# Scores over 512 keys on 64 partitions, and K transposed in halves, in a two-layer cached-attention decode kernel

## The chip, the cores and the metric

The kernel runs on one core of one Trainium2 chip. The metric is device time in microseconds (us), the median of several runs. Engines are named as the profile names them: PE is TensorE (PEld its weight loads), DVE is VectorE, ACT ScalarE, POOL GpSimd, SP SyncE, whose queue issues all the loads.

## The reference

One token of width 640 passes two equal layers, each an attention over a cache and a mixer. What the change touches is the attention's scores and softmax:

```python
Hq, Hkv, Sk, Dh = 32, 32, 32768, 192
W = min(4096, max(256, Sk // 4))                 # 4096 keys
q = (x @ wq).reshape(B, Sq, Hq, Dh)              # x after layernorm, one row
k = k_cache[:, :, Sk - W:, :]                    # bf16, 1.5 MB a head
v = v_cache[:, :, Sk - W:, :]
scores = einsum("bhqd,bhkd->bhqk", q, k) * Dh ** -0.5
p = softmax(scores, axis=-1)
o = einsum("bhqk,bhkd->bhqd", p, v)
x = x + o.reshape(B, Sq, Hq * Dh) @ wo
```

The mixer is layernorm, a product with w3, gelu and a product with w4 (for one token the shifted part of the reference is zero). Both layers read the same caches and weights.

## The kernel before

**Loads.** K and V of each head come as one load of 1.5 MB each into one of 12 cells in SBUF (`take`, `give`: a cell is free again when the work that reads it has been given). Loads go out in one fixed order (`layer_stream`, `need`) from SP; in the steady part up to eight are under way at once, and an issue waits for the landing of an earlier one or for its cell. wo, w3 and w4 use cells too. Layer 1 (layer 0 in the code) goes through the groups of four heads from the last to the first. Eight heads (0 to 7, `NKEEP`) keep their transposed K in cells for layer 2, which begins with them and loads no K for them.

**K transposed (L450).** K lies with keys on partitions, and TensorE needs Dh there. VectorE transposes 32x32 blocks of 4-byte words, so pairs of bf16. `transpose_quart` does a quarter of a head, 128x768 words; `T(h, half)` does two. The result goes to a kept cell, or to `area`, one cell that four quarters use in turn.

**Scores (L534).** `scores` multiplies the 16 columns of `Qblk` (four heads times four blocks of 32 rows, zero where another head's columns are) by the transposed K. Six products (three blocks of 64 of Dh, even and odd) add up in PSUM. Quarter q writes to partitions 32q to 32q+15, one strip of 32, over 256 columns: 24 matmuls a head, over two strips in turn for a half, over all four for a kept head. Four heads add into one tile of 128 partitions and 256 columns. Two such tiles lie beside each other in one PSUM bank (`ST_both`, `next_scores`), so that the scores of the next group are made while this group's softmax reads the other.

**Softmax steps.** `part_max` (L557) takes the maximum over the 256 columns, `turn_max` (L562) turns the 128 maxima into a row, `full_max` (L567, L572) reduces them to one per head and scales, `spread_max` turns that into a bias (L580, L583) and takes the exponential (L586) with its sums, `turn_p` (L591, L593) transposes the probabilities in 32x32 blocks, `swap` (L605, L608, L613) brings them to keys on partitions (PT) with 16 small matmuls and sums the denominators, and `recip` inverts those.

**Values.** `pv` (L655) makes 16 matmuls over the four strips per head; VectorE transposes the result (L662, `o_sb`), and `o_fold` (L669 to L675) sums it into the head's column of oT. `o_sb` is also the space of the softmax steps (`o_words`).

**Order.** The order on each engine is that in which the program is written; the semaphores between engines are placed by the framework. For a group, the prologue makes the first head of the next group: T of both halves with `part_max` between them, S of both halves with `turn_max` and `full_max` between, then the other steps, the query of the group after, and T of the second head. Then, for each head of this group, PV, T and S of one more head of the next group, and the fold. The last groups of a layer (`hurry`, `quick`) have the last softmax early. In layer 2's first group the steps stand between the kept heads' scores:

```python
between = [lambda: (turn_max(), full_max()), spread_max, turn_p, lambda: None]
for (q2, h2), step in zip(keep, between):
    for half in range(2):
        T(h2, half)
        S(h2, half, ST_n, q2)
    step()
```

For a kept head T does nothing, and S makes all 24 matmuls at once and gives the cell back.

Of the kernel before, what the change touches and what calls it, by code (L numbers as in the profile page):

```python
# [18 lines left out]
P = 128  # L19
# [40 lines left out]
def kernel(  # L60
# [30 lines left out]
    QT = QC // P  # L91
    NT = 4
    QUART = NFB * (NGK // NT) * P * 2
    FREE = NT * QUART
    scale = float(Dh) ** -0.5
# [336 lines left out]

    def transpose_quart(layer, h, q):

        if layer == 1 and h < NKEEP:
            return kept[h][:, q * QUART:(q + 1) * QUART]
        Kn = need("k", layer, h)
        NY = NFB * (NGK // NT)
        Ku = Kn[:].bitcast(U32).rearrange("p (j y b) -> p j y b", j=NJ4, b=32)
        if layer == 0 and h < NKEEP:  # L440
            if q == 0:
                kept[h] = take(("T", h))
            T = kept[h][:, q * QUART:(q + 1) * QUART]
        else:
            if area[0] is None:
                area[0] = take(("area", layer))
            T = area[0][:, area[1] * QUART:(area[1] + 1) * QUART]
            area[1] = (area[1] + 1) % NT
        Tu = T.bitcast(U32).rearrange("p (y j b) -> p j y b", y=NY, j=NJ4)
        nc.vector.transpose(Tu, Ku[:, :, q * NY:(q + 1) * NY])  # L450
        if q == NT - 1:
            give(("k", layer, h))
        return T

    def qproj_steps(c, xc, part=None, row=None):
# [29 lines left out]
        def spread():  # L485
            if row is not None:
                qT_ps = psm.tile([P, n], F32, tag="psm")
                for tl in range(n):
                    i, j = divmod(tl, n // 2)
                    nc.tensor.matmul(qT_ps[:, tl:tl + 1], lhsT=row[:, j * P:(j + 1) * P],  # L490
                                     rhs=Eq[0:33, i, 0:1], start=True, stop=True)
                held["q"] = qT_ps
            Xq = o_bytes[:, 2 * (SW + 2 * QH):][:, 0:4 * n].rearrange("p (t b) -> p t b", b=4)
            nc.vector.tensor_tensor(  # L494
                out=Xq[:], in0=held["q"][:, :].unsqueeze(2).broadcast_to([P, n, 4]),
                in1=maskq[:, :].unsqueeze(1).broadcast_to([P, n, 4]), op=ALU.mult)
            held["x"] = Xq
# [25 lines left out]

    def scores(h, Ts, q0, ST_ps, hq):

        ng = NGK // NT
        Q = [Qblk[:, h // QH % 2, QAT[hq] + n * QSTEP:][:, 0:QW] for n in range(NCOL)]
        views = [T.rearrange("p (g f i t) -> p g f i t", f=NFB, g=ng, i=P) for T in Ts]
        for f in range(NFB):
            for t in range(2):  # L530
                n = 2 * f + t
                for i, T4 in enumerate(views):
                    r = 32 * (q0 + i)
                    nc.tensor.matmul(  # L534
                        ST_ps[r:r + QW, :].rearrange("p (g i) -> p g i", g=ng), lhsT=Q[n],
                        rhs=T4[:, :, f, :, t],
                        start=(hq == 0 and n == 0), stop=(hq == QH - 1 and n == NCOL - 1))


    ST_both = psS.tile([P, 2 * SW], F32, name="ST_ps")  # L540
    nc.vector.memset(ST_both[:], 0.0)
    turn = [0]

    def next_scores():
        turn[0] += 1
        i = turn[0] % 2
        return ST_both[:, i * SW:(i + 1) * SW]

    def softmax_steps(n, ST_ps, sc, space, bank=None):
        held = {}
        halves = space.bitcast(BF16)

        def part_max():
            pm = short("pm")
            nc.vector.tensor_reduce(out=pm[:], in_=ST_ps, op=ALU.max, axis=AX.X)  # L557
            held["pm"] = pm

        def turn_max():  # L560
            pmT_ps = psm.tile([1, P], F32, tag="psm")
            nc.tensor.transpose(pmT_ps[0:1, :], held["pm"][:, 0:1], ident[:, :])  # L562
            held["pmT"] = pmT_ps

        def full_max():
            ngm = space[0:1, SW:SW + 2 * QH]
            nc.vector.tensor_reduce(out=ngm[:], in_=held["pmT"][0:1, :].rearrange("o (q x m) -> o x q m", q=4, m=NM),  # L567
                                    op=ALU.max, axis=AX.XY, negate=True)
            held["PrT"] = halves[:, SW:2 * SW]

            wide = held["PrT"][0:1, :].bitcast(F32)
            nc.vector.tensor_scalar(  # L572
                out=wide.rearrange("o (q x m) -> o q x m", q=4, m=NM),
                in0=ngm[:].unsqueeze(1).unsqueeze(3).broadcast_to([1, 4, 2 * QH, NM]),
                scalar1=sc[0:1, 0:1], scalar2=None, op0=ALU.mult)
            held["w"] = wide

        def spread_max():
            nb_ps = psm.tile([P, 1], F32, tag="psm")
            nc.tensor.matmul(nb_ps[:], lhsT=held["w"],  # L580
                             rhs=one[0:1, :], start=True, stop=True)
            nb_sb = space[:, 289:290]
            nc.scalar.copy(nb_sb[:], nb_ps[:])  # L583
            Pr = halves[:, 0:SW]
            lpart = space[:, 288:289]
            nc.scalar.activation(out=Pr, in_=ST_ps, func=ACTF.Exp,  # L586
                                 bias=nb_sb[:, 0:1], scale=sc[:, 0:1], accum_out=lpart[:, 0:1])
            held["Pr"], held["l"] = Pr, lpart

        def turn_p():  # L590
            nc.vector.transpose(held["PrT"], held["Pr"])  # L591
            lh = space[:, 280:284]
            nc.vector.tensor_scalar(out=lh[:], in0=hm[:], scalar1=held["l"][:, 0:1], scalar2=None, op0=ALU.mult)  # L593
            held["lh"] = lh

        def swap():
# [6 lines left out]
            for m in range(NM):  # L603
                for q in range(NT):
                    nc.tensor.matmul(PT_ps[32 * m:32 * (m + 1), :, :, ng * q:ng * (q + 1)], lhsT=Eq[:, q, :],  # L605
                                     rhs=src[:, m:QW:NM], start=True, stop=True)
# [4 lines left out]
            else:  # L611
                l_ps = bank[:, 512:512 + QH]
            nc.tensor.matmul(l_ps[:], lhsT=ones, rhs=held["lh"][:], start=True, stop=True)  # L613
            held["lps"] = l_ps
# [112 lines left out]
    def attention(layer, x_cur, rs_cur, x_new, z_new, rs_new, ss_new):  # L727
# [12 lines left out]

        def T(h, half):
            for q in (2 * half, 2 * half + 1):
                if (h, q) not in Th:
                    Th[h, q] = transpose_quart(layer, h, q)

        def S(h, half, ST_ps, hq):
            if layer == 1 and h < NKEEP:
# [3 lines left out]
                return  # L751
            scores(h, [Th.pop((h, q)) for q in (2 * half, 2 * half + 1)], 2 * half, ST_ps, hq)
            if half == 1 and layer == 0 and h == last_plain:
# [39 lines left out]
        for hq, h in enumerate(groups[0]):  # L793
            for half in range(2):
                if layer == 0:
                    T(h, half)
                else:
                    Th.update({(h, q): transpose_quart(layer, h, q) for q in (2 * half, 2 * half + 1)})
                S(h, half, ST, hq)
# [11 lines left out]
        def early_t(quarts):  # L811
            h, i = quarts.popleft()
            Th[h, i] = transpose_quart(layer, h, i)

# [321 lines left out]
```

## Time and profile before

| | |
|---|---|
| time, median of 3 runs | 511.49 us (511.09 to 511.76) |
| the profiled execution | 511.59 us, its span 509.8 us |
| PE busy | 317.2 us (62%), 4084 matmuls |
| DVE busy | 292.0 us (57%) |
| ACT busy | 48.9 us (10%) |
| read from HBM | 214.01 MB, 420 GB/s over the span |
| scores' matmuls (L534) | 1536 of 128x256, 365 ns each |
| K's transposes (L450) | 224 of 128x768 words, 945 ns each |
| TensorE clock granted, mean | 0.708 |

The span runs from the first instruction to the last. PE's busy time counts matmuls that run side by side once, and a matmul's own time holds its way through the array, so counts times means say little there. Where the text names a moment, it is in us from the span's start; layer 1 runs to about 286 us. In a row of the timeline the columns are start, length, engine, line, operation, operands and count; the bracket is the engine's idle time before it and what ended it.

### The profile page before, as it was taken

The page shows a single profiled execution, that of the slowest core. Times are in us where ns is not written, and L with a number is a line of the kernel's source. Part 1 is how long each engine was busy: PE and PEld are TensorE (multiplying, and loading weights), DVE is VectorE, ACT ScalarE, POOL GpSimd, SP SyncE. Part 2 cuts the span into 40 slices and gives each one's busy share as a digit, 9 for nine tenths or more (in the row PEclk, how much of TensorE's full clock was granted, in tenths as well). Part 3 has the DMA queues.
Part 4 walks back from the last instruction along what each step waited for, and adds up shares of the span by engine and source line. Part 5 has one row for each costly group of instructions (what it writes and reads, how often), then busy time and mean ns, then how long its engine had stood idle before and what let it go on. Part 6 is the DMA issues. An engine that isn't in the chain of part 4 may idle for free.

```text
span 509.8 us, 9498 instructions
## 1 busy us (share of the span) xinstructions
PE 317.2 (62%) x4084; PEld 188.0 (37%) x4084; DVE 292.0 (57%) x604; ACT 48.9 (10%) x173; POOL 3.7 (1%) x16
## 2 busy tenths in 40 slices
PE   1056677676566664767755777576565665657685
PEld 0023334334333332534433645343333333324354
DVE  2068557656774755566723276865575555756522
ACT  1000101010010100001010111010100101001111
POOL 2000000000000000000000000000000000000000
PEclk9999656557787776655675597957785967876655
DMA  9999999999999999999999999999999999999996
GB/s 370 432 432 430 429 441 432 437 429 419 420 426 433 432 427 448 432 404 459 422 396 414 370 435 429 443 429 440 426 422 424 429 422 432 428 446 429 415 409 246
DMA packets 12014, 214.63 MB, mean 421 GB/s; under 512 B 2564, under 2 KB 3076, under 8 KB 7428
## 3 DMA queue, kind: packets, MB, share of 16 engines
q1 hardware_dynamic: 11972, 214.02, 98.6%
q8 instruction: 32, 0.52, 0.4%
q14 instruction: 10, 0.08, 0.0%
HBM read 214.01 MB, written 0.00 MB: 420 GB/s over the span
## 4 chain that ended last, share of the span: by engine, by line
DMA 65%; PE 17%; DVE 12%; issue 3%; ACT 1%; SPq 1%; DVEq 0%; ACTq 0%
DMA cell<-in_A_k_cache_dram 43%; DMA cell<-in_A_v_cache_dram 18%; DVE cell L450 8%; PE ST_ps L534 8%; DMA cell<-in_B_w_dram 4%; PE O_ps L655 4%; DVE o_sb L662 1%; PE y_ps L1080 1%; DVE words L557 1%; PE qT_ps L480 1%; DVE V_ps L644 1%; PE nb_ps L580 1%; ACT o_sb L586 1%; PE l_ps L613 1%; SPq L55 0%
## 5 line engine op out<-in xcount | busy, mean ns | idle before, releaser
L534 PE MATMUL ST_ps<-cell,Qblk 128*16 128x256 bf16 x1536 | 158.2, 365 | 110.3 <-DVE cell L450 67.4
L450 DVE STREAM_TRANSPOSE cell<-cell 128x768 uint32<-128x768 uint32 x224 | 201.6, 945 | 33.4 <-DMA cell<-in_A_k_cache_dram 32.6
L534 PEld LDWEIGHTS <-Qblk 128*16 128x16 bf16 x1536 | 84.6, 108 | 176.7 <-issue 152.4
L655 PE MATMUL O_ps<-cell,PT 128*2 128x384 bf16 x968 | 94.8, 458 | 10.1 <-DMA cell<-in_A_v_cache_dram 8.2
L662 DVE STREAM_TRANSPOSE o_sb<-O_ps 128x384 f32<-128x384 f32 x62 | 35.4, 571 | 79.7 <-PE O_ps L655 79.7
L655 PEld LDWEIGHTS <-PT 128*2 128x2 bf16 x1024 | 43.6, 98 | 25.7 <-issue 17.7
L670 ACT ACTIVATE words<-oT_ps,words 32x6 bf16<-32x6 f32 x40 | 10.3, 257 | 163.3 <-PE oT_ps L669 151.5
L591 DVE STREAM_TRANSPOSE o_sb<-o_sb 128x256 bf16<-128x256 bf16 x15 | 6.7, 445 | 30.7 <-ACT o_sb L586 24.2
L669 PE MATMUL oT_ps<-o_sb,Lq 128*32 128x6 f32 x160 | 13.3, 192 | 10.0 <-DVE o_sb L662 9.4
L669 PEld LDWEIGHTS oT_ps<-o_sb,Lq 128*32 128x32 f32 x160 | 11.7, 137 | 18.5 <-issue 11.6
L675 ACT ACTIVATE words<-oT_ps,words 32x6 bf16<-32x6 f32 x24 | 6.2, 257 | 114.8 <-PE ST_ps L534 90.5
L494 DVE TENSOR_TENSOR o_sb<-qT_ps,words 128x24 bf16<-128x24 f32 (+1 forms) x18 | 3.0, 164 | 22.0 <-PE qT_ps L480 17.0
L480 PE MATMUL qT_ps<-words,wq_sb 128*128 128x1 bf16 x210 | 7.0, 165 | 13.0 <-DMA wq_sb<-in_A_wq_dram 12.1
L469 PE MATMUL qr_ps<-wq_sb,words 128*1 128x384 bf16 x90 | 13.6, 454 | 0.0
L480 PEld LDWEIGHTS <-wq_sb 128*128 128x128 bf16 x210 | 6.6, 100 | 14.2 <-DMA wq_sb<-in_A_wq_dram 13.2
L583 ACT COPY o_sb<-nb_ps 128x1 f32<-128x1 f32 x15 | 2.4, 159 | 93.3 <-PE nb_ps L580 93.3
L605 PEld LDWEIGHTS <-ident 128*32 128x32 bf16 x256 | 5.9, 113 | 12.2 <-issue 12.0
L701 PE MATMUL yr_ps<-cell,words 128*1 128x320 bf16 x108 | 10.0, 325 | 0.0
L674 PE MATMUL oT_ps<-o_sb,Lq 128*32 128x6 f32 x48 | 6.1, 200 | 6.0 <-DVE o_sb L673 5.8
L674 PEld LDWEIGHTS oT_ps<-o_sb,Lq 128*32 128x32 f32 x48 | 5.5, 143 | 10.5 <-issue 9.7
L580 PEld LDWEIGHTS nb_ps<-words,o_sb 1*128 1x128 f32 x30 | 6.6, 273 | 6.4 <-issue 5.6
L683 PE MATMUL y_ps<-words,cell 128*128 128x1 bf16 x210 | 7.1, 166 | 2.5 <-issue 1.4
(161 smaller groups left out, 205.6 us busy)
## 6 DMA issues: line engine op xcount, KB each, us to landing
cell<-in_A_k_cache_dram SPq DMA_DIRECT2D x56, 1536.0 KB, 27.7
cell<-in_A_v_cache_dram SPq DMA_DIRECT2D x56, 1536.0 KB, 27.7
cell<-in_A_wo_dram SPq DMA_DIRECT2D x13, 960.0 KB, 27.7
wq_sb<-in_A_wq_dram SPq DMA_DIRECT2D x5, 1536.0 KB, 13.4
cell<-in_A_v_cache_dram SPq DMA_DIRECT2D x6, 768.0 KB, 23.6
cell<-in_B_w_dram SPq DMA_DIRECT2D x1, 1536.0 KB, 11.8
cell<-in_B_w_dram SPq DMA_DIRECT2D x2, 768.0 KB, 10.3
cell<-in_A_wo_dram SPq DMA_DIRECT2D x3, 480.0 KB, 17.0
```

The source lines that it names most:

```text
L450: nc.vector.transpose(Tu, Ku[:, :, q * NY:(q + 1) * NY])
L469: nc.tensor.matmul(qr_ps[32 * i:32 * i + 1, :], lhsT=xc[:, kc:kc + 1], rhs=wq_sb[:, kc, t0 * P + i * N:t0 * P + (i + 1) * N], start=(kc == ...
L480: nc.tensor.matmul(qT_ps[:, tl:tl + 1], lhsT=wq_sb[:, kc, t * P:(t + 1) * P], rhs=xc[:, kc:kc + 1], start=(kc == 0), stop=(kc == ND - 1))
L534: nc.tensor.matmul(ST_ps[r:r + QW, :].rearrange("p (g i) -> p g i", g=ng), lhsT=Q[n], rhs=T4[:, :, f, :, t], start=(hq == 0 and n == 0), s ...
L580: nc.tensor.matmul(nb_ps[:], lhsT=held["w"], rhs=one[0:1, :], start=True, stop=True)
L655: nc.tensor.matmul(O_ps[r:r + 2, :], lhsT=PT[:, hq, 2 * i:2 * i + 2], rhs=v_pair(V, h, 2 * i * Dh, 2 * Dh), start=(i < 4), stop=(i >= NB - 4))
L662: nc.vector.transpose(o_sb[:], O_ps.rearrange("p (e a c) -> p e c a", e=2, c=NA))
L669: nc.tensor.matmul(oT_ps[r, :], lhsT=Lq[:], rhs=o_sb[:, e, :, e], start=(e == 0), stop=(e == 1))
L670: nc.scalar.activation(oT[r, :], oT_ps[r, :], ACTF.Copy, scale=rl[r, 0:1])
L674: nc.tensor.matmul(oT_ps[r, :], lhsT=Lq[:], rhs=o2, start=True, stop=True)
L683: nc.tensor.matmul(y_ps[:, n:n + 1], lhsT=wo_t[:, k * D + n * P:k * D + (n + 1) * P], rhs=oT[:, k:k + 1], start=(i == 0), stop=(i == len(o ...
L701: nc.tensor.matmul(yr_ps[32 * i:32 * i + 1, :], lhsT=oT[:, k:k + 1], rhs=wo_t[:, k * D + i * N:k * D + (i + 1) * N], start=(k == 0), stop= ...
```

## The change

A head's K is transposed in two halves of 128x1536 words (`transpose_half`, `NT = 2`) where it was four quarters of 128x768. A half's scores are six matmuls of 512 columns to one strip of 32 PSUM partitions, where they were twelve of 256 columns over two strips; a kept head has twelve over two strips, where it had 24 over four. A group's scores lie on 64 partitions and 512 columns. The two score tiles take turns on the upper and the lower 64 partitions of the bank (`HP`), where they took turns on its left and right columns. The softmax steps follow: half the partitions, twice the columns; `turn_p` writes to the other 64 partitions of its space, the scaled maxima (`wide`) have words of their own, and `swap` has eight matmuls for 16. `early_t` is called for two halves instead of four quarters.

```diff
-    NT = 4
-    QUART = NFB * (NGK // NT) * P * 2
-    FREE = NT * QUART
+    NT = 2
+    HP = P // 2
+    HALF = NFB * (NGK // NT) * P * 2
+    FREE = NT * HALF
...
-                    r = 32 * (q0 + i)
+                    r = ST[0] + 32 * (q0 + i)
                     nc.tensor.matmul(
-                        ST_ps[r:r + QW, :].rearrange("p (g i) -> p g i", g=ng), lhsT=Q[n],
+                        ST_both[r:r + QW, :].rearrange("p (g i) -> p g i", g=ng), lhsT=Q[n],
...
-    ST_both = psS.tile([P, 2 * SW], F32, name="ST_ps")
+    ST_both = psS.tile([P, SW], F32, name="ST_ps")
...
     def next_scores():
         turn[0] += 1
-        i = turn[0] % 2
-        return ST_both[:, i * SW:(i + 1) * SW]
+        i = turn[0] % 2 * HP
+        return i, ST_both[i:i + HP, :]
...
+        at, ST_ps = ST
+        S, T = slice(at, at + HP), slice(HP - at, P - at)
...
-            pmT_ps = psm.tile([1, P], F32, tag="psm")
-            nc.tensor.transpose(pmT_ps[0:1, :], held["pm"][:, 0:1], ident[:, :])
+            pmT_ps = psm.tile([1, HP], F32, tag="psm")
+            nc.tensor.transpose(pmT_ps[0:1, :], held["pm"][S, 0:1], ident[S, S])
...
+            wide = space[0:1, 306:306 + HP]
...
-            nc.tensor.matmul(nb_ps[:], lhsT=held["w"],
+            nc.tensor.matmul(nb_ps[S, :], lhsT=held["w"],
                              rhs=one[0:1, :], start=True, stop=True)
...
+            held["PrT"] = halves[T, 0:SW]
             nc.vector.transpose(held["PrT"], held["Pr"])
...
-                    nc.tensor.matmul(PT_ps[32 * m:32 * (m + 1), :, :, ng * q:ng * (q + 1)], lhsT=Eq[:, q, :],
+                    nc.tensor.matmul(PT_ps[32 * m:32 * (m + 1), :, :, ng * q:ng * (q + 1)], lhsT=Eq[T, (HP - at) // 32 + q, :],
                                      rhs=src[:, m:QW:NM], start=True, stop=True)
...
-            for q in (2 * half, 2 * half + 1):
-                if (h, q) not in Th:
-                    Th[h, q] = transpose_quart(layer, h, q)
+            if (h, half) not in Th:
+                Th[h, half] = transpose_half(layer, h, half)
...
-            scores(h, [Th.pop((h, q)) for q in (2 * half, 2 * half + 1)], 2 * half, ST_ps, hq)
+            scores(h, [Th.pop((h, half))], half, ST_ps, hq)
```

## The prediction

> **What bounds the kernel now.** I read the page first, its slices above all:
>
> ```profile
> PEclk9999656557787776655675597957785967876655
> DMA  9999999999999999999999999999999999999996
> ```
>
> The DMA row is full from the first slice to the last but one: the time is 214 MB over one saturated set of queues, and engine work costs nothing until it makes a load start late. The clock row shows TensorE granted half speed in places (the 5s) and full speed in others; the mean is 0.708. So I looked for places where a load waits for compute. The chain of waits, in order of time:
>
> ```profile
> 48.09 0.32 DVE words L557
> ...
> 77.59 0.32 DVE words L557
> ...
> 79.91 27.70 DMA cell<-in_A_v_cache_dram
> ...
> 137.22 0.32 DVE words L557
> ...
> 168.64 0.32 DVE words L557
> ...
> 201.54 0.32 DVE words L557
> ...
> 234.14 0.32 DVE words L557
> ...
> 245.99 10.64 DMA cell<-in_A_v_cache_dram
> ...
> 263.48 7.29 DMA cell<-in_A_v_cache_dram
> ```
>
> L557 (`part_max`) opens each group of four heads, so its starts are the group's cycle. In layer 1 it is 29.50 us at first and 29.8 over the two cycles from 77.59 to 137.22, then 31.42, 32.90 and 32.60. The DMA rows say how much is queued. A load issued at 79.91 lands after 27.70 us, and 1.5 MB loads land 3.64 us apart, so some 24 us of loads stand ahead of it. At 245.99 it is 10.64 - 3.64 = 7.0, at 263.48 (0.94 MB, 2.28 us) 5.0. Compute may be late by that much, less the start of a transfer (I allow 1.5 us), before the queues run dry: some 22 us in mid-layer, 3.5 us at the end of layer 1, where the kept cells leave few buffers.
>
> How close compute runs to the DMA shows in VectorE's waits for K. In the timeline there are none over 0.8 us from 48 to 166, and then these:
>
> ```profile
> 166.80 1.84 DVE L450 STREAM_TRANSPOSE cell<-cell 128x768 uint32<-128x768 uint32 x2 [2.01 <-DMA cell<-in_A_k_cache_dram]
> ...
> 190.24 3.56 DVE L450 STREAM_TRANSPOSE cell<-cell 128x768 uint32<-128x768 uint32 x4 [0.84 <-DMA cell<-in_A_k_cache_dram]
> ...
> 199.71 1.84 DVE L450 STREAM_TRANSPOSE cell<-cell 128x768 uint32<-128x768 uint32 x2 [3.05 <-DMA cell<-in_A_k_cache_dram]
> ...
> 380.64 1.84 DVE L450 STREAM_TRANSPOSE cell<-cell 128x768 uint32<-128x768 uint32 x2 [3.25 <-DMA cell<-in_A_k_cache_dram]
> ...
> 390.11 1.84 DVE L450 STREAM_TRANSPOSE cell<-cell 128x768 uint32<-128x768 uint32 x2 [1.85 <-DMA cell<-in_A_k_cache_dram]
> ```
>
> So layer 1's chain VectorE - TensorE - VectorE takes 29.4 us of a 31.4 us DMA cycle, 2 us from setting the pace. Layer 2 has 5.1 us to spare (3.25 + 1.85).
>
> **The scores' matmuls.** The timeline has them at both clocks, for two and for four strips of 32 PSUM partitions:
>
> ```profile
> 288.01 1.46 PE L534 MATMUL ST_ps<-cell,Qblk 128*16 128x256 bf16 x24 [0.28 <-DVE Qblk L518]
> ...
> 299.05 0.86 PE L534 MATMUL ST_ps<-cell,Qblk 128*16 128x256 bf16 x24
> ```
>
> ```profile
> 137.59 1.45 PE L534 MATMUL ST_ps<-cell,Qblk 128*16 128x256 bf16 x12 [2.17 <-DVE words L557]
> ...
> 307.32 0.85 PE L534 MATMUL ST_ps<-cell,Qblk 128*16 128x256 bf16 x12
> ```
>
> Twelve over two strips take as long as 24 over four: strips run side by side, and the time is that of one strip's six matmuls. Half clock less full clock is 0.60 us for 6*256 columns: 0.39 ns a column at full clock, and 0.25 us fixed. After the change a half of K goes to one strip, as six matmuls of 512 columns: 0.25 + 1.20 = 1.45 us at full clock, 2.65 at half. That is +0.6 or +1.2 us per half of a head, though the instructions are halved; for a kept head (two strips instead of four) the same. The other strips idle meanwhile, and two halves overlap only when both are ready.
>
> [...]
>
> **The other parts.** VectorE transposes take 0.445 us for 256 elements (L591), 0.571 for 384 (L662), 0.945 for 768 (L450): 0.975 ns an element and 0.2 fixed. Four of 768 in a row took 3.51, so each removed one saves 0.11: 0.9 us a group, 0.1 to 0.2 per head on the chain. A fused one should take 1.70. The softmax steps halve their partitions and double their elements: L557 from 0.38 to 0.65, the P transpose from 0.45 to 0.70, the exponential (0.56) by 0.25 to 0.35: +0.8 us on the way to PT. L605's 16 matmuls (0.45 us) become eight: -0.2. `wide` in words of its own, L567, L572, the bias and l matmuls keep their number and are under 0.6 us each; I count 0. `early_t` has two calls for four, under the PVs of layer 2's first group. No load changes place on SP; each waits for a cell that S, T or PV gives back.
>
> The two slots of `area` stay: T into one waits for the S that read it. At half clock a slot turns in 1.70 + 2.65 = 4.35 us where K lands every 3.64: up to 2 us late in the first group, inside 24 us of queue; left to the range.
>
> **One group in layer 1, on its chain.** The prologue's `S(h0,0)`, `turn_max`, `S(h0,1)`, bias, exponential, P transpose, swap, PV stand in one order. At half clock both S count: 1.2 + 1.2 + 0.8 - 0.3 = +2.9. At full clock the transpose of h0's second half covers most of the first S: 0.6 + 0.8 - 0.45 = +0.95. Head h1: its S runs between two PVs; +1.2 at half clock, at full clock mostly under VectorE's work, +0.3. Heads h2 and h3: after the last transpose the second half's S is left, PV's matmuls of that strip queue behind it, and o_sb's transpose and the next head's K behind PV: +1.2 - 0.1 each, or +0.5. Sum: +6.3 at half clock, +2.25 at full, the two bounds. From 48 to 201 the clock was full a third of the time. Longer S streams keep TensorE busier, so I take half the time: +4.3 us a group, less 0.4 for the old work.
>
> **The sum.** From 48.09 to 201.54 are five cycles, 153.45 us with 2.01 + 0.84 + 3.05 = 5.9 of waiting in them. After: 147.55 + 5*3.9 = 167, 13.6 us late. The next cycle adds 3.5, the one with the last scores (234 to 255) 2.5: near 20 us late where the load of 263.48 is issued. TensorE's wait for V at 256.67 (0.85) takes up 1, the queue 3.5: some 15 us of dry queues. If S need not wait for readers of the other half of its bank (below), the prologue's two S overlap and this is about 11. I take 11.5, towards that end since layer 1 stays near the DMA's pace only by a few us.
>
> Layer 2: eight kept heads cost 2*1.2 + 6*0.6 = +6 us from 288 to 300, less what stands under softmax steps. The loads issued there follow the kept heads' S by 1.2 to 6 us more, and find 3.5 to 8 us of loads ahead: nothing lost. Later cycles have 5.1 us of room for 4, and 24 us of queue for the lateness. At the end the second S before the last PT (478.5 to 480.1) and its softmax are late by 1.2 + 0.8; TensorE's wait for w3 at 503.0 (0.93) and for wo cover all but 0.5. Sum +12: the profiled execution, 511.59 (span 509.8 and 1.8 around it), becomes 523.6; the median of the three runs is 0.1 lower: **523.5 us**.
>
> **A wait that may go.** S of the next group waits for readers of the other half of its bank, at 137.59 for L557 (above), and here for the exponential:
>
> ```profile
> 297.69 0.86 PE L534 MATMUL ST_ps<-cell,Qblk 128*16 128x256 bf16 x24 [0.94 <-ACT o_sb L586]
> ```
>
> After, the two score tiles lie on different partitions of the bank. If order is kept by bank and partitions, the waits go: 0.4 to 0.6 us a group, 1.5 us in the kept stretch, and at half clock up to 1 us of overlap. If by bank, they grow with L557 and the exponential by 0.3 each. No row decides.
>
> [...]
>
> **Rivals.**
> 1. The clock answers: longer streams hold TensorE at full speed three quarters of the time or more. Then +2.25 to 3 a group fits 31.4 - 29.4 plus the gain on old work, layer 1 is some 5 us late at 263, 1 to 2 us are lost, and 1 at the end: 512.8 to 515. For: clock 1.00 from 292 to 308, where TensorE is dense. Against: from 60 to 112 the windows read mostly 0.50 with PE busy 68%.
> 2. The queue hides it all, or six matmuls of 512 take what six of 256 do, so that PE's part is unchanged: 510.6 to 512.5. Against: the 2 us of room a cycle.
> 3. Faster: the freed waits outweigh S at full clock, and layer 2's first loads (289 to 300) start 1 to 2 us earlier. It decides only if DMA engines idle there: slice 23 of the page reads 370 GB/s beside some 430, but its packets sum to under 0.5 us of idle time, and the end is set by w4's landing; at most 1.5 us: 510.
> 4. The clock stays as before or lower: +5 to 6 a group, 25 to 30 us late, 20 to 25 lost: 530 to 536.
>
> **How the numbers follow.** The forecast (515 to 530) has 0.60, rival 1 0.20, rival 2 0.08, rival 3 0.04, rival 4 0.08. 0.2% is 1 us, about what a measurement of this kernel tells from no change. Faster by more: 0.04; within: 0.07; slower: 0.89. The range takes in rival 1 and half of rival 4: 513 to 533.
>
> **What would show it.** L534: 768 matmuls of 128x512, six in about 1.45 or 2.65 us. L450: 112 of 128x1536 near 1.70 us. L557's cycles in layer 1 at 33 to 34 us, no VectorE wait for K at 166 and 199, issue-to-landing under 20 us before 200, DMA slices under 9 between 200 and 290, more 6s to 8s in the clock row. I am wrong if six 512-column matmuls take under 1 us, if layer 1's cycles stay at 31.4 us, or if the queues stay full to 280.

## The result, and the profile after

The changed kernel takes 536.04 us (median of six runs, 533.27 to 536.94), the kernel before 511.61 (511.09 to 511.81): 1.0469 times as long, 95% interval 1.0445 to 1.0493. The direction was as forecast, the size was not: +24.4 us against +12, and outside the range that ended at 533. The profiled execution took 534.84 us, with a span of 533.1, 23.3 more than before.

The same two rows of the page, in 40 slices (13.3 us each):

```profile
PEclk9987677877768777778895579787889877986955
DMA  9999999999999998868699999999999999999996
```

The DMA row, full before, has a hole in slices 15 to 19 (200 to 267 us), and the clock row shows 7s and 8s where it had 5s and 6s. How deep the hole is shows in the table of windows; its columns are the stretch, its length, the busy time of each engine, then the granted clock, the DMA's share and GB/s. First the kernel before, cut at the first group's `part_max`, the sixth's and the load of 263.48:

```profile
48.09:201.54 153.45, 98.69 (x1086) 55.33 (x1086) 97.02 (x181) 15.22 (x50) 0.00 (x0) 0.67 1.00 431
201.54:263.48 61.94, 43.30 (x520) 26.59 (x520) 37.01 (x70) 5.30 (x20) 0.00 (x0) 0.61 0.99 425
263.48:509.80 246.32, 159.09 (x2314) 96.89 (x2313) 137.63 (x308) 26.31 (x98) 0.71 (x2) 0.70 0.98 415
```

Then the kernel after, where the same load goes out at 285.12:

```profile
48.09:201.54 153.45, 104.41 (x743) 39.37 (x742) 89.63 (x135) 15.01 (x46) 0.00 (x0) 0.74 1.00 427
201.54:285.12 83.58, 56.53 (x498) 24.58 (x493) 48.09 (x62) 6.95 (x24) 0.00 (x0) 0.83 0.84 325
285.12:533.10 247.98, 176.82 (x1866) 81.94 (x1865) 140.59 (x260) 27.77 (x98) 0.71 (x2) 0.78 0.98 410
```

Up to 201 us the queues stay full although compute is already late. The second stretch takes 83.58 us where it took 61.94: 21.6 of the 23.3 us are lost here, at 325 GB/s for 425. Layer 2 takes 1.7 us more, at the same DMA share of 0.98. So the loss is the one that the prediction looked for, at the place it named.

The chain of waits gives the cycle: L561 is `part_max` now.

```profile
51.37 0.70 DVE words L561
84.67 0.65 DVE words L561
118.70 0.71 DVE words L561
152.84 0.66 DVE words L561
186.94 0.71 DVE words L561
220.90 0.66 DVE words L561
254.96 0.71 DVE words L561
276.96 0.69 DVE words L561
```

The cycles are 33.30, 34.03, 34.14, 34.10, 33.96 and 34.06 us and a short one of 22.00, where they were 29.4 to 32.9 and 20.7. They are strikingly equal, which matters below. The groups of instructions show the parts (line, operation, shapes and count, then busy us and mean ns of one):

```profile
L535 PE MATMUL ST_ps<-cell,Qblk 128*16 128x512 bf16 x768 | 225.8, 500 | 88.3 <-DVE cell L451 50.6 <-DVE words L561 31.4 <-DVE o_sb L676 3.8
L451 DVE STREAM_TRANSPOSE cell<-cell 128x1536 uint32<-128x1536 uint32 x112 | 195.0, 1756 | 14.6 <-DMA cell<-in_A_k_cache_dram 8.2 <-PE ST_ps L535 3.4 <-PE O_ps L658 2.3
L561 DVE TENSOR_REDUCE words<-ST_ps 64x1 f32<-64x512 f32 x16 | 10.8, 674 | 2.2 <-PE ST_ps L535 2.1
```

A fused transpose takes 1.756 us (forecast 1.70), `part_max` 0.67 (0.65); from the page's groups, the exponential takes 0.774 (0.81 to 0.91) and P's transpose 0.706 (0.70). TensorE's idle time ahead of scores is led by K's transposes (50.6 us) and by `part_max` (31.4 us): that second wait is the one that was hoped to go. In the timeline, one group's opening:

```profile
153.53 2.71 PE L535 MATMUL ST_ps<-cell,Qblk 128*16 128x512 bf16 x6 [1.96 <-DVE words L561]
156.18 0.26 PE L566 MATMUL pmT_ps<-ident,words 64*1 64x64 f32 x1
156.37 2.73 PE L535 MATMUL ST_ps<-cell,Qblk 128*16 128x512 bf16 x6
```

The first S starts when `part_max` has read the other tile, on other partitions of the same bank. The second stands behind `turn_max` in TensorE's order, and the two follow each other at 2.7 us each: the price that was forecast for half clock (2.65).

### The profile page after: what moved, and what is told of

Same layout as the page of the kernel before. It is cut to its first block, busy times and chain, and to the rows that moved or that the text cites. A ratio compares the mean times of both kernels' runs of the same rounds, so it can differ in the third digit from the quotient of the medians.

```text
span 533.1 us, 7567 instructions
## 1 busy us (share of the span) xinstructions
PE 356.1 (67%) x3188; PEld 152.8 (29%) x3188; DVE 296.2 (56%) x492; ACT 51.8 (10%) x173; POOL 3.7 (1%) x16
## 4 chain that ended last, share of the span: by engine, by line
PE 39%; DMA 34%; DVE 18%; issue 5%; ACT 3%; SPq 1%; ACTq 0%
PE ST_ps L535 26%; DMA cell<-in_A_v_cache_dram 16%; DMA cell<-in_A_k_cache_dram 14%; DVE cell L451 10%; PE O_ps L658 7%; DMA cell<-in_B_w_dram 4%; DVE o_sb L665 3%; ACT o_sb L588 2%; DVE words L561 1%; DVE o_sb L594 1%; PE y_ps L1082 1%; PE PT_ps L608 1%; PE l_ps L616 1%; DVE wx_sb L714 1%; PE qT_ps L481 1%
## 5 line engine op out<-in xcount | busy, mean ns | idle before, releaser
L535 PE MATMUL ST_ps<-cell,Qblk 128*16 128x512 bf16 x768 | 225.8, 500 | 88.3 <-DVE cell L451 50.6
L451 DVE STREAM_TRANSPOSE cell<-cell 128x1536 uint32<-128x1536 uint32 x112 | 195.0, 1756 | 14.6 <-DMA cell<-in_A_k_cache_dram 8.2
L535 PEld LDWEIGHTS <-Qblk 128*16 128x16 bf16 x768 | 67.0, 103 | 211.2 <-issue 177.5
L658 PEld LDWEIGHTS <-PT 128*2 128x2 bf16 x1024 | 35.9, 86 | 30.4 <-issue 16.2
L594 DVE STREAM_TRANSPOSE o_sb<-o_sb 64x512 bf16<-64x512 bf16 x15 | 10.6, 706 | 42.7 <-ACT o_sb L588 42.7
L672 PE MATMUL oT_ps<-o_sb,Lq 128*32 128x6 f32 x160 | 12.7, 187 | 11.1 <-DVE o_sb L665 10.5
L672 PEld LDWEIGHTS oT_ps<-o_sb,Lq 128*32 128x32 f32 x160 | 10.4, 128 | 19.8 <-issue 13.9
L481 PE MATMUL qT_ps<-words,wq_sb 128*128 128x1 bf16 x210 | 7.0, 164 | 13.2 <-DMA wq_sb<-in_A_wq_dram 12.3
L495 DVE TENSOR_TENSOR o_sb<-qT_ps,words 128x24 bf16<-128x24 f32 (+1 forms) x18 | 2.9, 162 | 22.1 <-PE qT_ps L481 19.4
L561 DVE TENSOR_REDUCE words<-ST_ps 64x1 f32<-64x512 f32 x16 | 10.8, 674 | 2.2 <-PE ST_ps L535 2.1
L588 ACT ACTIVATE o_sb<-ST_ps,o_sb,words 64x512 bf16<-64x512 f32 x15 | 11.6, 774 | 0.5
L502 PE MATMUL Qrep_ps<-o_sb,Lb 128*128 128x24 bf16 (+1 forms) x18 | 3.2, 177 | 11.6 <-DVE o_sb L495 11.6
L519 DVE TENSOR_TENSOR Qblk<-Qrep_ps,words 128x48 bf16<-128x48 f32 (+1 forms) x36 | 5.5, 192 | 8.1 <-PE Qrep_ps L502 7.9
L608 PEld LDWEIGHTS <-ident 64*32 64x32 bf16 x128 | 3.2, 94 | 23.3 <-issue 20.8
```

The costliest lines, as they stand in the source:

```text
L481: nc.tensor.matmul(qT_ps[:, tl:tl + 1], lhsT=wq_sb[:, kc, t * P:(t + 1) * P], rhs=xc[:, kc:kc + 1], start=(kc == 0), stop=(kc == ND - 1))
L535: nc.tensor.matmul(ST_both[r:r + QW, :].rearrange("p (g i) -> p g i", g=ng), lhsT=Q[n], rhs=T4[:, :, f, :, t], start=(hq == 0 and n == 0), ...
L561: nc.vector.tensor_reduce(out=pm[S, :], in_=ST_ps, op=ALU.max, axis=AX.X)
L588: nc.scalar.activation(out=Pr, in_=ST_ps, func=ACTF.Exp, bias=nb_sb[:, 0:1], scale=sc[S, 0:1], accum_out=lpart[:, 0:1])
L658: nc.tensor.matmul(O_ps[r:r + 2, :], lhsT=PT[:, hq, 2 * i:2 * i + 2], rhs=v_pair(V, h, 2 * i * Dh, 2 * Dh), start=(i < 4), stop=(i >= NB - 4))
L672: nc.tensor.matmul(oT_ps[r, :], lhsT=Lq[:], rhs=o_sb[:, e, :, e], start=(e == 0), stop=(e == 1))
```

## The experiments

### Which part of the change, and which layer

**Layer 1 alone, layer 2 alone.** Both forms in one kernel, chosen by layer (the rest of the diff only keeps the two sets of functions side by side):

```diff
-    new = 0        # layer 1 alone
+    new = 1        # layer 2 alone
...
         two = layer == new
```

> The changed form of scores, softmax and K's transposes in layer 1 only; layer 2 as before. Theory (one strip's stream of 512 columns lengthens the chain of each group of layer 1 past the DMA's cycle): layer-1 cycles near 34 us as in the changed kernel, first load of V after the gap some 20 us late, and a time of 531 to 535, that is 20 to 23 us of the 24.4 lost. Rival (the kept heads of layer 2, where softmax steps stand between scores, carry the loss): 512 to 516.

Measured: 533.44 us, ratio 1.0422 (1.0373 to 1.0471).

> The changed form in layer 2 only; layer 1 as before, with K turned in quarters into the same places. Theory: layer 2 has room, so 511 to 514 (at most the 1.7 us that the changed kernel loses after the end of layer 1). Rival (kept heads carry the loss): 525 or more.

Measured: 514.29 us, ratio 1.0037 (1.0017 to 1.0056). Layer 1 carries 21.3 us, layer 2 2.1 (each against the 512.18 beside it), together nearly the change's 24.4; layer 2 came out 0.3 us above the stated range. Layer 2, with its kept heads, is the small part of the loss.

**K in halves alone**, scores and softmax as before:

```diff
-        nc.vector.transpose(Tu, Ku[:, :, q * NY:(q + 1) * NY])
+        nc.vector.transpose(Tu, Ku[:, :, q * NY:(q + 2) * NY])
```

> The kernel before with K turned in halves (one transpose of 1536 elements for two of 768), scores, strips and softmax as before. Theory: 511 to 513: a fused transpose saves 0.1 to 0.15 us of VectorE and gives S its first quarter 0.8 us later, both inside layer 1's 2 us a cycle. Rival (the halves make the chain longer, since S of the first quarter no longer starts under the second's transpose): 518 or more.

Measured: 511.89 us, ratio 0.9997 (0.9982 to 1.0011): nothing.

**The exponential twice**, in the kernel before, for the longer softmax steps:

```diff
-            nc.scalar.activation(out=Pr, in_=ST_ps, func=ACTF.Exp,
+            for _ in range(2):
+                nc.scalar.activation(out=Pr, in_=ST_ps, func=ACTF.Exp,
```

> The kernel before with the exponential issued twice, 0.56 us more on the way from scores to PT in each group, for the change's longer softmax steps (+0.75 us by the two traces: part_max, exponential and P's transpose). Theory: 511 to 513, within layer 1's room of 2 us a cycle. Rival (the softmax steps carry the loss): 522 or more.

Measured: 513.41 us, ratio 1.0010 (0.9994 to 1.0026): 0.4 us above the stated range and not told from nothing.

**Half of the products**, in the changed kernel:

```diff
-            for t in range(2):
+            for t in range(1):
```

> The changed kernel with three of the six products of each half head (it leaves out t=1, half of the scores' sum over Dh): a strip's stream is as long as before the change, all else is the change. Theory: 512 to 517, layer-1 cycles 31 to 32 us. Rival (softmax steps or transposes): still 530 or more, since these are untouched.

Measured: 512.25 us, ratio 0.9997 (0.9980 to 1.0013). With the softmax on 64 partitions, the fused transposes, the score tiles in halves of a bank and the new order all in place, the whole loss is gone once a strip's stream is as short as before. The length of the stream is necessary for every microsecond of it. The granted clock was lower here (0.59 between 50 and 250 us, for 0.75 in the change and 0.65 before), and still nothing was lost: a low clock without the long stream cost nothing.

**512 columns as twice 256**, in the changed kernel:

```diff
-                    nc.tensor.matmul(
-                        ST_both[r:r + QW, :]...
-                        rhs=T4[:, :, f, :, t],
+                    for g in (0, 2):
+                        nc.tensor.matmul(
+                            ST_both[r:r + QW, g * P:(g + 2) * P]...
+                            rhs=T4[:, g:g + 2, f, :, t],
```

> The changed kernel with each scores matmul of 512 columns cut into two of 256, on the same strip. Theory (a strip's time goes with its columns): 535 to 539, twelve in 2.7 to 3.0 us at half clock. Rival (512 columns are slower than two times 256, or the fixed cost of an instruction counts): under 530, or over 542.

Measured: 538.13 us, ratio 1.0507 (1.0484 to 1.0529). Twelve of 256 take what six of 512 do. Its cycles in layer 1 go with the clock: 33.1 to 34.3 us where it is full for 0.50 to 0.52 of the time, one of 30.18 us at 0.89 and one of 37.62 at 0.36. In its timeline:

```profile
119.25 2.72 PE L536 MATMUL ST_ps<-cell,Qblk 128*16 128x256 bf16 x12 [2.10 <-DVE words L562]
121.90 0.26 PE L567 MATMUL pmT_ps<-ident,words 64*1 64x64 f32 x1
122.09 2.73 PE L536 MATMUL ST_ps<-cell,Qblk 128*16 128x256 bf16 x12
```

### Is the length of the stream enough?

**All scores twice**, in the kernel before, so that a strip's stream is as long as in the change and all else is as before:

```diff
-                    nc.tensor.matmul(
-                        ST_ps[r:r + QW, :]...
+                    for again in range(2):
+                        nc.tensor.matmul(
+                            ST_ps[r:r + QW, :]...
```

> The kernel before with each scores matmul issued twice in a row (the scores come out doubled): a strip's stream is as many columns as in the change, but the softmax steps, the transposes and the bank's halves stay as before. Theory: the length of the strip's stream is what counts, so 528 to 537, layer-1 cycles 33.5 to 34.5 us. Rivals: the softmax steps on half the partitions, or K's fused transposes, carry the loss: 511 to 515; the number of instructions matters beside the columns (48 a head against 24): above 540.

Measured: 526.76 us (524.66 to 531.73), ratio 1.0285 (1.0218 to 1.0352): below the range.

**Scores twice in layer 1, for one, two and four heads of a group** (the same loop, with `range(2 if now[0] == 0 and hq == 2 else 1)`, `hq >= 2` and no condition on `hq`):

> The kernel before, with the scores matmuls issued twice in layer 1 for one head of each group of four (hq = 2; its scores come out doubled). Theory with the room that the prediction read (2 us a cycle): one head adds at most 1.2 to 2.4 us at half clock, so at most a fraction of 1 us a cycle past the DMA's, taken up by the queue: 511 to 513. Rival (no room in layer 1 at all, each us of chain counts): 515 to 520.

> As the run with one head doubled, for two heads of each group (hq = 2 and 3) in layer 1. Theory with 2 us of room a cycle: 2 to 4 us of chain more, 0.5 to 1.5 us a cycle past the DMA's: 513 to 521. Rival (no room): 521 to 527; rival (room is larger, only the prologue's scores count): 511 to 512.

> As the run with one head doubled, for all four heads of each group in layer 1; layer 2 as before. Theory: within 2 us of the run that doubles all scores in both layers, since layer 2 has room. Rival (layer 2 counts): over 5 us below that run.

Measured: one head 512.98 us (ratio 1.0006, 0.9985 to 1.0027), two 514.0 (1.0019, 1.0001 to 1.0038), four 520.88 (518.24 to 524.5; 1.0126, 1.0059 to 1.0193). One and two heads fit the room of 2 us a cycle: TensorE does more, and the time hardly moves until the chain reaches the DMA's cycle. With four the layer loses 8.3 us (3 to 10 by the interval): not the 21 of the change. By the medians it is also 5.9 us under the run that doubles both layers, as the rival (layer 2 counts) said; but each of the two spreads over 6 to 7 us, and their profiled executions, 524.50 and 524.69 us, do not show the difference. What doubled scores cost in layer 2 stays open.

So the length of the stream is necessary, but in this form it brings only two to three fifths of the loss (8.3 of 21.3 us in layer 1, 14.6 of 24.4 in both layers). What else differs is in the cycles. In the two kernels with doubled scores they come in two kinds (`part_max` to `part_max`, and the share of the cycle at full clock, from the clock's records):

| kernel | cycles in layer 1, us (share at full clock) |
|---|---|
| changed | 33.30 (0.41), 34.03 (0.50), 34.14 (0.50), 34.10 (0.50), 33.96 (0.50), 34.06 (0.60) |
| doubled, both layers | 31.20 (0.66), 30.85 (0.77), 34.13 (0.50), 30.87 (0.79), 30.44 (0.78), 33.83 (0.60) |
| doubled, layer 1 | 33.10 (0.51), 31.09 (0.77), 30.85 (0.77), 34.13 (0.50), 30.63 (0.79), 34.10 (0.60) |

At a share of 0.50 a doubled cycle takes 34.13 us, like the change's 34.0 to 34.1; at 0.77 it takes 30.9 and costs nothing, since the DMA needs 31.4 (31.42 us from 137.22 to 168.64 before). In the traces of the kernel before and of the changed one every record of the clock (64 and 76 of them) reads 0.5 or 1.0 and lasts 3.41 us or a multiple of it, but for the last, which ends with the execution. 34.13 us is ten such windows, 30.7 is nine. Windows cut along them show how the two keep their clocks (columns as above; the second number is PE's busy time, the last three the clock, the DMA's share and GB/s). The changed kernel:

```profile
166.20:169.62 3.42, 3.42 (x28) 1.55 (x28) 0.94 (x6) 0.26 (x1) 0.00 (x0) 0.50 0.97 417
169.62:173.03 3.41, 1.08 (x7) 0.35 (x5) 2.86 (x3) 0.00 (x0) 0.00 (x0) 1.00 1.00 432
173.03:176.44 3.41, 3.41 (x25) 1.06 (x22) 1.10 (x2) 0.00 (x0) 0.00 (x0) 0.50 1.07 461
176.44:179.86 3.42, 1.09 (x9) 0.34 (x5) 2.45 (x3) 0.26 (x1) 0.00 (x0) 1.00 1.02 436
179.86:183.27 3.41, 3.41 (x22) 1.16 (x21) 1.50 (x2) 0.00 (x0) 0.00 (x0) 0.50 1.08 461
183.27:186.68 3.41, 1.34 (x14) 0.48 (x10) 2.19 (x3) 0.52 (x2) 0.00 (x0) 1.00 0.97 418
```

The doubled scores (both layers), at the same place of a cycle:

```profile
160.44:163.85 3.41, 2.50 (x59) 1.75 (x55) 1.52 (x5) 0.26 (x1) 0.00 (x0) 1.00 1.09 470
163.85:167.26 3.41, 2.11 (x30) 1.37 (x31) 3.20 (x5) 0.00 (x0) 0.00 (x0) 1.00 1.10 466
167.26:170.68 3.42, 1.98 (x40) 1.40 (x37) 1.40 (x3) 0.26 (x1) 0.00 (x0) 1.00 1.00 431
170.68:174.09 3.41, 2.64 (x40) 1.82 (x41) 2.67 (x5) 0.00 (x0) 0.00 (x0) 1.00 1.04 447
```

In the change a head takes two windows. In one, at half speed, TensorE is busy throughout with S and PV, and the next is granted full speed; in that one it is done after a third (1.08 of 3.41 us), stands while VectorE turns the next head's two halves (2.86 us of VectorE), and the next is at half speed again. The doubled scores have the same columns on each strip but twice the strips and four times the instructions (48 a head for 12); TensorE is busy for 1.98 us or more of each of these windows, and full speed is kept.

The traces of all the kernels here bear this out. Up to 280 us they hold 205 windows at full speed in which TensorE is busy for under 1.4 us, and the window after each of them is at half speed (13 of 13 in the kernel before, 17 of 17 in the changed one); of 307 with 2 us or more, 285 are followed by full speed (2 of 3 and 12 of 13).

### Two causes, each taken away

**Idle-time matmuls**, 24 of 128 columns behind each head's PV in layer 1, in the changed kernel:

```diff
+    def keep_busy(n):
+        for i in range(n):
+            nc.tensor.matmul(V_bank[0:32, VW:VW + P], lhsT=Lb[:, 0:32], rhs=Lb[:, 0:P], start=True, stop=True)
...
                 pv(layer, h, hq, PT, steps[3] if quick and hq == 3 else fold)
+                if layer == 0 and nxt0:
+                    keep_busy(24)
```

> The changed kernel with 24 idle-time matmuls of 128 columns (their result is read by nobody) behind each head's PV in layer 1, where TensorE stands 2.3 us for K's next transpose. New theory, the clock: in the changed kernel TensorE alternates window by window (3.41 us at half speed, fully busy; 3.41 us at full speed, a third busy), and a group takes ten such windows, 34.1 us; with the same strips' streams the doubled scores stayed at full speed for four or five windows in a row and took nine, 30.7 us. If so, more work on TensorE makes the kernel faster: granted clock above 0.85 in layer 1, cycles 30.5 to 31.5 us, 512 to 518. Rival (length of the chain alone, the clock as it is): the filling delays S, cycles 35 us or more, 540 or more.

Measured: 527.78 us, ratio 1.0304 (1.0279 to 1.0329): 672 useless matmuls make the changed kernel 8 us faster. The windows show why (same columns):

```profile
168.58:171.99 3.41, 2.91 (x49) 1.93 (x48) 1.18 (x4) 0.26 (x1) 0.00 (x0) 1.00 1.00 432
171.99:175.40 3.41, 1.99 (x12) 0.64 (x12) 2.94 (x3) 0.00 (x0) 0.00 (x0) 1.00 0.97 418
175.40:178.82 3.42, 2.62 (x49) 1.87 (x48) 1.64 (x3) 0.52 (x2) 0.00 (x0) 1.00 0.80 345
178.82:182.23 3.41, 1.70 (x8) 0.64 (x8) 3.33 (x4) 0.00 (x0) 0.00 (x0) 1.00 1.06 452
```

The heads' part of the cycle now runs at full speed. The openings still read 0.50 for a window or two, and the cycles are 30.8 to 32.8 us with one of 34.7. The theory had the direction and the clock (0.90 between 50 and 250 us); that the clock was the whole rest was too much by some 10 us. The rival (filling only lengthens the chain) falls.

**Twelve instead of 24:**

> As the run with 24, with 12 such matmuls a head. Clock theory: between, some cycles nine windows and some ten: 513 to 530. Rival (chain alone): 536 to 542.

Measured: 535.22 us, ratio 1.0454 (1.0418 to 1.0491), not told from the change. Its cycles are mixed, as expected (31.33 us at a share of 0.78, 34.39 at 0.50), but too few are short. The time is 5 us above the stated range and within 1 us of the rival's: a dose too small buys nothing that shows.

**The same 24 in the kernel before:**

> The kernel before with the same 24 matmuls behind each head's PV in layer 1. If the DMA sets the time of the kernel before, as the prediction read it, a clock of 0.85 or more in layer 1 brings nothing: 511 to 513. Rival (before was held by TensorE's clock too): under 510. Rival (filling delays the chain): over 515.

Measured: 514.18 us, ratio 1.0038 (1.0024 to 1.0052), 1.2 us above the first range. Two cycles fall to 28.6 and 28.5 us, the second at full clock for 0.96 of its time, and the later ones are 31.5 to 32.7 as before: TensorE's speed brought nothing here (514.18 us for 512.24), where the DMA set the pace.

**Two banks for the score tiles**, in the changed kernel:

```diff
+    two = ST_both[:, :], V_bank[:, 1536:2048]
...
-        return i, ST_both[i:i + HP, :]
+        bank = two[turn[0] % 2]
+        return i, bank[i:i + HP, :], bank
...
-            b = V_bank[:, i:i + n].bitcast(U32)
+            at = i % 1536
+            b = V_bank[:, at:at + n].bitcast(U32)
```

> The changed kernel with the two score tiles in two banks of PSUM, on their halves of the partitions as in the change (the last of the four pieces of V that are kept in PSUM between the layers lies over the first, so one head's PV in layer 2 reads some wrong words). It takes away the wait of a group's first S for part_max of the group before (1.96 us at 153.53) that the prediction hoped to see go. If that wait is what the prediction missed: 2 us a group less, 522 to 530. If the alternating clock fixes the group at ten windows, the 2 us are given back further on: 533 to 537, unless the shift lets the clock stay up.

Measured: 528.30 us (526.61, 527.65, 528.95 and 535.28), ratio 1.0355 (1.0280 to 1.0430). In its timeline the first S of a group waits for its own K alone, and starts as `part_max` does (146.47):

```profile
146.60 2.72 PE L535 MATMUL V_ps<-cell,Qblk 128*16 128x512 bf16 x6 [1.39 <-DVE cell L451]
149.25 0.26 PE L570 MATMUL pmT_ps<-ident,words 64*1 64x64 f32 x1
149.44 1.64 PE L535 MATMUL V_ps<-cell,Qblk 128*16 128x512 bf16 x6
```

The second S also finds a faster clock here (1.64 us, for 2.73 at 156.37). Three of its cycles are 30.6 to 31.1 us, three stay at 33.6 to 34.4. Two banks were worth 7.7 us by the medians, 2 to 10 by the interval. The wait on the bank is only part of the 1.96 us: the transposed half is there when `part_max` starts, so S could start 0.6 us sooner (0.13 us after it, for 0.69 at 153.53), some 4 us over layer 1. The short cycles are at full clock for 0.66 of the time and the long ones for 0.50, so the rest came with the clock.

**The opening's order alone**, with the wait left in:

```diff
                     S(h0, 0, ST_n, 0)
+                    S(h0, 1, ST_n, 0)
                     turn_max()
                     full_max()
-                    S(h0, 1, ST_n, 0)
```

> The changed kernel with turn_max and full_max put behind the second S of a group's first head, so that this S needs not stand behind part_max's turn on TensorE and both strips can stream together. Theory: the two S of the prologue overlap by up to 2.7 us at half clock where the wait on the bank allows it, the turned maximum comes later by as much as S lasts: net gain 0 to 2 us a group, 520 to 536. Rival (the prologue's order is not what costs, the second half of h0 is late by its transpose anyway): 535 to 540.

Measured: 537.07 us, ratio 1.0482 (1.0447 to 1.0517): the rival. Its cycles are 33.35 and then 33.96 to 34.20, ten windows again. The two S do overlap:

```profile
155.12 4.40 PE L535 MATMUL ST_ps<-cell,Qblk 128*16 128x512 bf16 x12 [1.96 <-DVE words L561]
```

Counted from the start of `part_max`, both are done after 5.1 us where the change took 6.3, but the exponential starts after 6.35 for 6.60: the turned maximum now waits for both S, and most of the gain is given back at once.

**Both repairs, then more filling in the opening** (two banks and `keep_busy(24)` behind PV; then a further `keep_busy(24)` ahead of `turn_p`):

> The changed kernel with both repairs: two banks for the score tiles and 24 idle-time matmuls behind each head's PV in layer 1 (two of the four pieces of V kept in PSUM lie over the other two, so one head's PV in layer 2 reads some wrong words). Alone they gave back 7.7 and 8.3 us of 24.4. Theory (two separate causes, the wait on the bank and the granted clock): they add up, 518 to 523, layer-1 cycles 31 to 32 us. Rival (both act only through the clock): no better than the better one alone, 526 to 529.

> As the run with both repairs, with 24 more such matmuls in each group's opening of layer 1, behind the output row's matmuls, where TensorE stands 1.6 us for VectorE and the window after reads half speed. Clock theory: the clock stays above 0.9 in layer 1: 513 to 520, below the run with both repairs. Rival (the opening's chain is lengthened by the filling): the same or up to 3 us above it.

Measured: 524.48 us (ratio 1.0223, 1.0177 to 1.0269) and 521.36 (1.0185, 1.0139 to 1.0231). Together the repairs give back 11.6 us by the medians, between the sum of the two (16) and the better one alone: neither range was met. They may act in part on the same thing, the clock; the interval of two banks is too wide to show it. With the opening filled as well, 14.7 of 24.4 are back; the intervals of the two runs overlap. The last one is 1.4 us above its range. Its cycles take 31.12, 30.90, 32.72, 30.85, 31.24, 33.33 and 22.97 us, at full clock for 0.79 to 0.89 of the time in the first six. These seven sum to 213.15 where before had 254.76 - 48.02 = 206.74; and the first group is 4.2 us late (52.20 for 48.02). 6.4 and 4.2 make its 10 us. What is left I put down to the longer stream itself, since half of the products lost nothing; no run takes it apart further. No version here beats the kernel before.

### What lateness costs

One load can be followed through the kernels with a visible loss, the one that went out at 263.48 before. How late it goes out, and how much longer the same profiled execution took than 511.59:

| kernel | load late, us | execution longer, us |
|---|---|---|
| before, idle-time matmuls | 3.5 | 2.5 |
| changed, both repairs and opening | 10.2 | 10.2 |
| doubled, layer 1 | 11.5 | 12.9 |
| changed, both repairs | 11.9 | 13.9 |
| changed, two banks | 13.2 | 15.0 |
| changed, idle-time matmuls | 15.3 | 16.1 |
| changed, 12 idle-time matmuls | 21.7 | 23.0 |
| changed, layer 1 alone | 21.9 | 21.6 |
| changed | 21.6 | 23.3 |
| changed, 512 columns as twice 256 | 23.6 | 25.9 |
| changed, order of the opening | 25.3 | 27.4 |

From 10 us on, the lateness at that load is paid in full, to within 0.3 us less and 2.3 more. (The doubled scores of both layers, 8.5 late and 13.1 longer, lose more in layer 2.) No cushion is left at this point. The DMA rows of the changed kernel from 255 to 290 us, in 40 slices of 0.875 us, show why:

```profile
DMA  9091000098090909099694969697996978887969
GB/s 786 0 861 56 0 0 0 0 562 337 0 899 0 899 0 899 0 449 449 281 562 169 581 225 506 281 358 316 386 702 260 562 337 358 386 351 176 255 281 340
```

Hardly a packet starts from about 258 to 262: a load of 1.5 MB goes out at 261.08, its first packet starts 1.34 us later (the prediction allowed 1.5 for this), and only then does the work go on. The loads that stand ahead of 285.12 were all issued after this gap, each 21.4 to 22.1 us late as well. It is not the first gap: matched one by one with the kernel before, every load from the one issued at 195.31 (175.54 before) to this one went out 19.6 to 22.7 us late, about where the DMA row first falls under 9.

## Why the prediction was right or wrong

**Right.** The bound (DMA before, compute after, the loss between 200 and 285); the strip's stream as the cause (half of the products: nothing lost; layer 1 alone: 21 of 24); 2.65 us for six matmuls at half clock (2.71) with the number of instructions of no account; the transposes and softmax steps, by size and as harmless in themselves; the room of 2 us a cycle (one or two doubled heads of four: at most 1.5 us); full clock for half of the time (0.50). Rival 2 falls with the same row: 2.71 us for six is 0.45 us each. At full clock (1.00 in this stretch) six take 1.52 us, 0.25 us each, for 1.45 forecast:

```profile
258.50 1.52 PE L535 MATMUL ST_ps<-cell,Qblk 128*16 128x512 bf16 x6
```

**The sum, term by term** (profiled executions):

| step of the prediction | forecast, us | measured, us |
|---|---|---|
| first group, `area` slots | left out ("up to 2") | 51.37 - 48.02 = 3.35 |
| five cycles to 201.47 | 13.6 | 220.90 - 201.47 - 3.35 = 16.1 |
| next two cycles | 3.5 + 2.5 | 276.96 - 254.76 - 19.4 = 2.8 |
| late at 254.76 | near 20 | 22.2 |
| V's wait and the queue | -4.5 | load 21.64 late: -0.6 |
| S free of the other half's readers | towards -4 | 0; S still starts behind `part_max` |
| layer 2 and the end | +0.5 | 23.25 - 21.64 = 1.6 |
| sum | 12 | 23.25 |

The lateness was nearly right (20 for 22.2), although its parts were not: the five cycles take 33.9 us each (for 33.4) and the first group's delay, set aside as hidden in 24 us of queue, stays in the lateness all the way. Half of the products brought the first `part_max` to 47.06, so it belongs to the stream too.

**The step that failed is the deduction**, "takes up 1, the queue 3.5" and "I take 11.5, towards that end": 8.5 us taken off of which 0.6 came. Left whole, the 20 us and layer 2's 0.5 would have given 532. The 3.5 us were read as loads standing ahead of 263.48. They do, and the same load still finds as much ahead of it after the change, 7.21 us from issue to landing for 7.29:

```profile
285.12 7.21 DMA cell<-in_A_v_cache_dram
```

But these loads are released by the same late chain and move with it. The stock had been used up once, at about 200 us. A stock can be spent against lateness once, at the load where it is first short; the same stock cannot be deducted again at a later load.

The other part was a choice between two bounds where "no row decides", and the text leaned to the free one. No run shows a free order within one bank, on which the 4 us from 15 to 11 rest. In this kernel the order was kept for the whole tile in its bank: S starts 0.05 us after `part_max` ends (153.53 for 152.84 + 0.64), on other partitions; whether the tile or the bank sets this order, no run tells apart. The run with two banks shows what the hope was worth: 7.7 us by the medians, some 4 of it by the earlier start and the rest with the clock.

**The rivals.** Rival 4's time (530 to 536) came about, but not by its mechanism: the clock between 50 and 250 us was not lower but higher (0.75 for 0.65). The clock of rival 1, which answers longer streams, was nearly reached in the kernels with doubled scores (full in layer 1 for 0.67 and 0.70 of the time), though not its time, and not in the change: the same columns per strip, in a quarter of the instructions of the doubled scores, left TensorE idle for two thirds of every second window. Rival 3 (faster) falls with the wait that stayed. The prediction weighed the clock as an average; what decided in these traces was how much work a window of 3.41 us held (1.08 us at 169.62 in the change, then half speed; 1.98 or more from 160.44 in the doubled scores, and full speed).

**Open:** the exact amount of work in a window that keeps full speed (between 1.4 and 2.6 of 3.41 us busy both happen: 1.66 kept it in one place, 1.86 lost it in another, and the ends of matmuls are modelled); what holds the cycle at ten windows so evenly; and what doubled scores cost in layer 2.

## What to carry to other kernels

Count a queue's stock once: find the first load where lateness exceeds what is queued, and from there on pass the lateness through whole, because the loads that seem to stand ahead later are late themselves. When a change narrows a matmul's output to fewer strips, price it by the columns of one strip at both clocks (here 1.52 and 2.71 us for six matmuls of 512), and look at TensorE's busy time window by window rather than at its mean: the chain here that alternated between a full window (3.41 us) and one that was a third busy (1.08) did most of its work at half clock. Two score tiles that shared an allocation and a PSUM bank were one resource to this program's order, even on different partitions (S 0.05 us after `part_max` ended): take such tiles for one until a run shows otherwise.

## What the runs showed of the hardware that was not expected

- TensorE's granted clock changed only after 3.41 us or a multiple of it (64 records in the trace of before, 76 in that of the changed kernel), and in the changed kernel it settled into a lock with the work: five groups in a row took 33.96 to 34.14 us, ten windows, at full speed for 0.50 to 0.60 of the time.
- 24 useless matmuls a head made the kernel 8.3 us faster (536.04 to 527.78); twelve made no difference that shows (535.22).
- Matmuls of 512 and of 256 columns cost the same per column on one strip here: six took 2.71 us and twelve 2.72 at half clock.
- After a window of 3.41 us at full speed with under 1.4 us of TensorE work, the next was at half speed each time (205 of 205 in the traces of this case, up to 280 us; 30 of 30 in those of before and after alone).
